# Attention scores of two steps issued together, with the low half of the queries in pairs of 64-row matmuls

## The chip, the cores and the metric

One core of one Trainium2 chip. The time is device microseconds of the whole program, the median of several runs. TensorE (PE in the profile) does the matmuls, its weight loads are shown as PEld, VectorE is DVE, ScalarE is ACT, GpSimd is POOL, and SP is the engine whose queue issues every DMA of this kernel.

## The reference

Three stages in a row. Squared-ReLU attention over two sequences of 3008 rows, then two feed-forward layers of 256 x 2048 x 256 over the 6016 rows:

```python
scores = (1/S) * z @ z.T                  # z: (2, 3008, 64)
attn = maximum(scores, 0) ** 2
x = u * (attn @ v)                        # u, v: (2, 3008, 256)
h = x @ w_in;  g = P(h) / (Q(|h|) + 1e-6) # rational, cubic over quadratic
y = g @ w_out
h = y @ w2_in; out = maximum(0.01 * h, h) @ w2_out
```

The weights arrive as 64-bit floats, and the kernel turns them into 32-bit ones itself.

## The kernel before

Every product is made in fp32r, with each operand split into a high part and a low part (the remainder), so that a product is the sum of two or three matmuls.

**Steps.** Attention runs in steps `t`. A block `i` of 512 queries (448 for the last of a sequence) takes 12 steps, one for each pair of 128-key blocks; there are 12 blocks, so 144 steps, and `t = 12 i + pair`. In one turn of the loop the program issues `scores(t)` (four matmuls of 512 columns on PE, then Relu and Square on ACT: tiles `sc`, `r` or `extra`, `ph`), then `av(t - 2)` (twelve matmuls, tile `oT`), then on DVE `square(t)` (line 232: r = r*r) and `square_low(t)` (line 238: the low part `pl`), and then the tasks that were registered for step `t`. The order on each engine is the order in which the program is written. The PSUM tile `sc` has two buffers, `r` and `ph` three, `pl` two.

**Keys and queries.** z has 64 columns. `prep_z` transposes 1024 rows of z on PE into a tile with the 64 columns twice, on partitions 0 to 63 and 64 to 127; ACT copies it (line 141) and DVE replaces the lower half by the remainder (line 142). So a key block holds the high part on one half of the partitions and the low part on the other. `prep_sq(i)` builds the queries of block `i` out of those keys by four DMAs (line 187): `queries[., 0]` holds the high part on both halves, `queries[., 1]` the low part on both halves. `scores` multiplies the key block (128 partitions) once by each. `first_z` does this for the first 512 rows, without DMAs.

**Tasks between the steps.** `prep_sq(i)` is registered for step 12 i - 4, `load_u`/`prep_u` (transposes `uTp` of u on PE, line 207, and a copy on ACT, line 209) for steps 12 i + 6 and 12 i + 10. The 32 pieces of weights are converted one every 3.4 steps, each over several steps from `s0 = 3 + k*17//5`: `load_w(k)` at step s0 - 1 (a DMA on SP, lines 279 and 282), `conv1` at s0 + 1 (ACT, line 287, and POOL), `conv2` to `conv4` at s0 + 2 to s0 + 4 (DVE, lines 294 to 303), `conv5` at s0 + 5 (ACT, line 315, POOL, line 316, and for the second layer's weights a store on SP, line 318). From step m0 = 119 on, the steps are merged with the first feed-forward layer; after step 145 only the two layers run.

The lines that tie the tasks to the steps:

```python
at(i * NPAIR - 4, lambda i=i: prep_sq(i))
...
halves = [(2 * (k // 16) + k % 2, (k % 16) // 4, (k % 4) // 2) for k in range(32)]
for k in range(32):
    s0 = 3 + k * 17 // 5
    for dt, f in ((-1, load_w), (1, conv1), (2, conv2), (3, conv3), (4, conv4), (5, conv5)):
        at(s0 + dt, lambda f=f, k=k: f(k))
```

By this rule `load_w(23)` stands at step 80 and `load_w(30)` at step 104, each right behind a `prep_sq` of the same step, and their `conv1` at steps 82 and 106.

Of the kernel before, what the change touches and what calls it, by code (L numbers as in the profile page):

```python
# [12 lines left out]
AF = mybir.ActivationFunctionType  # L13
ALU = mybir.AluOpType
# [3 lines left out]
def f32(ap):  # L18
    return ap.bitcast(F32)
# [3 lines left out]
def squared_relu_attention_moe_moe2(  # L23
# [14 lines left out]
    pe, act, dve, pool, sp = nc.tensor, nc.scalar, nc.vector, nc.gpsimd, nc.sync  # L38
# [4 lines left out]
    P = 128  # L43
    QB = 512
# [3 lines left out]
    NPAIR = KB // 2  # L48
# [3 lines left out]
    blocks = []  # L52
# [12 lines left out]
    def big(name):  # L65
        return ps.tile([P, 2, QB], F32, tag="big", name=name)
# [7 lines left out]
    def idle_acc(i, name):  # L74
        return acc(1 - own_acc(i), name)
# [43 lines left out]
    def key_chunk(c):  # L119
        return keys[c // 2][:, c % 2, :]  # L120

    def load_z(b, c, k0=0, k1=8):
# [7 lines left out]
                    sp.dma_start(t[h * KTAIL : (h + 1) * KTAIL, f1 - f0, d, :], z[b, f1 * P : S, :])  # L130
        return t

    def turn_z(pf, t, n):
        for k in range(n):
            pe.transpose(pf[:, k * P : (k + 1) * P], t[:, k, :, :].rearrange("p a d -> p (a d)"), ident)

    def prep_z(b, c, t, i):
        pf = idle_acc(i, f"zT{b}_{c}").rearrange("p a b -> p (a b)")
        turn_z(pf, t, 8)
        m = key_chunk(c)  # L140
        act.activation(m, pf, AF.Copy)
        dve.tensor_tensor(out=m[64:, :], in0=pf[64:, :], in1=f32(m[64:, :]), op=ALU.subtract)  # L142

    def first_z(ts):
        pf = idle_acc(0, "zT0_0").rearrange("p a b -> p (a b)")
        pg = big("zT0_0b").rearrange("p a b -> p (a b)")
        m, q = key_chunk(0), queries[0]
        for _ in range(WARM):
            pe.matmul(pg[:, :P], ident, ident, start=True, stop=True)
        turn_z(pf, ts[0], 4)  # L150
        act.activation(q[:, 0, :], pf[:, :QB], AF.Copy)
        turn_z(pg, ts[1], 4)
        dve.tensor_tensor(out=m[64:, :QB], in0=pf[64:, :QB], in1=f32(q[64:, 0, :]), op=ALU.subtract)
        act.activation(m[:64, :QB], f32(q[:64, 0, :]), AF.Copy)
        dve.tensor_tensor(out=q[:, 1, :], in0=pf[:, :QB], in1=f32(q[:, 0, :]), op=ALU.subtract)
        act.activation(m[:, QB:], pg[:, :QB], AF.Copy)
        dve.tensor_tensor(out=m[64:, QB:], in0=pg[64:, :QB], in1=f32(m[64:, QB:]), op=ALU.subtract)

    def load_v(b, c):
        t = raw_slot(f"vraw{b}_{c}", (P, 4, D))  # L160
# [20 lines left out]
    def prep_sq(i):  # L181
        b, q0, n = blocks[i]
        o = q0 % 1024
        m = key_chunk(q0 // 1024)[:, o : o + n]
        for h in range(2):
            for d in range(2):
                sp.dma_start(f32(queries[i % 2][d * 64 : (d + 1) * 64, h, :n]), f32(m[h * 64 : (h + 1) * 64, :]))

    uraw, uT, pacc = {}, {}, {}

# [21 lines left out]
    xs = [tc.dram_tile([P, 2, blocks[i][2]], F32, name=f"xs{i}") for i in range(NB)]  # L212
    R, PH, PL = {}, {}, {}

    def scores(t):
        i, pr = divmod(t, NPAIR)
        b, q0, n = blocks[i]
        s = big(f"sc{t}")
        for e in range(2):
            kb = 2 * pr + e  # L220
            o = (kb % 8) * P
            m = key_chunk(kb // 8)[:, o : o + P]
            for h in range(2):
                pe.matmul(s[:, e, :n], m, queries[i % 2][:, h, :n], start=h == 0, stop=h == 1)  # L224
        r = (extra[0] if t % 3 == 2 else slot(t % 3, f"r{t}"))[:, :, :n]
        act.activation(r, s[:, :, :n], AF.Relu, scale=SCALE)  # L226
        ph = slot(4 + t % 3, f"ph{t}", F32R)[:, :, :n]
        act.activation(ph, r, AF.Square)  # L228
        PH[t], R[t] = ph, r
# [99 lines left out]
    def at(step, f):  # L329
        tasks.setdefault(step, []).append(f)  # L330
# [49 lines left out]
    def load_x(i):  # L380
        n = blocks[i][2]
        if i >= 2 and i % 2 == 0:
            m = rtile(8, f"x1_{i}")
            xh, xl = (m[:, k, :].rearrange("p (a b) -> p a b", a=2) for k in range(2))
        else:
            xh, xl = slot(11, f"x1h{i}", F32R), slot(9, f"x1l{i}", F32R)
        sp.dma_start(f32(xl[:, :, :n]), xs[i])
        X1[i] = (xh, xl)
# [187 lines left out]
    TAIL = NC - NP  # L576
    MERGED = NP + 1
    m0 = NT + DEPTH - 3 * MERGED
    at(m0 - 4, lambda: load_x(0))
    at(m0 - 2, lambda: split_x1(0))  # L580
    at(m0 - 1, lambda: split_x1_low(0))
# [7 lines left out]
    for t in range(NT + DEPTH):  # L589
        c, ph = divmod(t - m0, 3)  # L590
        c = c if t >= m0 and c < MERGED else None
        if t < NT:
            scores(t)
        if c is not None and ph == 0:
            m1_h(c)
        if c and ph == 1:
            m1_y(c - 1, (0, 1, 2))
        if t >= DEPTH:
            av(t - DEPTH)
        if t < NT:  # L600
            square(t)
        if c is not None and ph == 0:
            m1_tb(c)
            m1_s(c)
            m1_v(c)
            m1_w(c)
            m1_q(c)
        if t < NT:
            square_low(t)
        for f in tasks.pop(t, []):  # L610
            f()
        if c is not None and ph == 1:
            m1_r(c)
            if c == NP:
                split_x2(0)
            m1_gh(c)
            m1_back(c)
        if c is not None and ph == 2:
            m1_gl(c)
# [97 lines left out]
```

## Time and profile before

| | |
|---|---|
| median of 3 runs | 1607.09 us (1605.28 to 1607.85) |
| the profiled execution | 1606.98 us, of which the span of its instructions is 1605.2 us |
| mean granted TensorE clock | 0.997 of 2.4 GHz |
| PE / DVE / ACT / POOL busy | 1581.3 / 1438.3 / 1098.6 / 165.4 us |
| attention alone (steps 0 to 118) | the first 457 us of the span |
| steps merged with the first layer | about 457 to 590 us |

The busy time of PE is a union of matmuls whose ends are modelled, so 100% does not say that it issues at its full rate; the distance between the starts of two groups does. A wait is shown in brackets behind the instruction that waited, with what released it. SPq rows are the DMA issues on the SP queue, with the time that the issue took on SP.

### The profile page before, as it was taken

How to read it: one execution, taken by the hardware profiler on the slowest of the kernel's cores; microseconds unless marked ns; L12 is line 12 of the kernel's file. 1: busy time of each engine (PE TensorE's matmuls, PEld its weight loads, DVE VectorE, ACT ScalarE, POOL GpSimd, SP SyncE). 2: the span in 40 equal slices, each digit the busy share in tenths (PEclk: the TensorE clock that was granted, in tenths of full speed). 3: DMA queues.
4: the chain of work that ended last, by engine and by line, in shares of the span. 5: the costliest groups of instructions: out<-in, count | busy, mean ns of one | idle time of the engine just before them, and what ended most of it. 6: DMA issues, size and time to landing. Idle time of an engine off the chain costs nothing.

```text
span 1605.2 us, 17951 instructions
## 1 busy us (share of the span) xinstructions
PE 1581.3 (99%) x7140; PEld 1323.7 (82%) x7140; DVE 1438.3 (90%) x1231; ACT 1098.6 (68%) x1109; POOL 165.4 (10%) x86
## 2 busy tenths in 40 slices
PE   8999999999999999999999999999999999999998
PEld 6788888788878887888888888888888888888887
DVE  7999999999979989999999998899999999999852
ACT  6666666666667766677777677777767676777643
POOL 2433335433200000000000000000000000000000
PEclk9999999999999999999999999999999999999999
DMA  6223236343220132000000000000000000000000
GB/s 170 66 67 87 84 90 178 115 137 119 92 68 23 56 113 104 13 14 14 14 1 12 13 13 14 13 14 13 12 14 14 13 14 1 25 1 0 14 1 25
DMA packets 51555, 74.42 MB, mean 46 GB/s; under 512 B 15632, under 2 KB 35344, under 8 KB 50448
## 3 DMA queue, kind: packets, MB, share of 16 engines
q1 hardware_dynamic: 51472, 73.28, 14.8%
q8 instruction: 56, 0.92, 0.2%
q14 instruction: 27, 0.22, 0.0%
HBM read 46.93 MB, written 20.71 MB: 42 GB/s over the span
## 4 chain that ended last, share of the span: by engine, by line
PE 85%; DVE 11%; issue 2%; ACT 2%; DMA 1%; DVEq 0%; POOL 0%; POOLq 0%; ACTq 0%
PE h L418 31%; PE y L432 31%; PE oT L257 16%; PE sc L224 5%; DVE pl L238 3%; DVE r L232 2%; DVE extra L232 1%; PE y L538 1%; DVE extra L303 1%; DVE extra L299 0%; PE uTp L207 0%; DVE t L464 0%; DVE extra L298 0%; DVE keys L142 0%; DVE t L459 0%
## 5 line engine op out<-in xcount | busy, mean ns | idle before, releaser
L432 PE MATMUL y<-gh,w 128*128 128x512 f32 (+1 forms) x1536 | 374.2, 386 | 0.7 <-DVE gh L475 0.5
L432 PEld LDWEIGHTS y<-gh,w 128*128 128x128 f32 x1536 | 288.2, 188 | 55.0 <-PE h L418 0.9
L257 PE MATMUL oT<-ph,V 128*128 128x512 f32 (+1 forms) x1128 | 276.3, 387 | 0.0
L257 PEld LDWEIGHTS oT<-ph,V 128*128 128x128 f32 x1128 | 212.9, 189 | 40.4
L432 PE MATMUL y<-gl,w 128*128 128x512 f32 (+1 forms) x768 | 203.3, 386 | 2.1 <-DVE gl L514 1.9
L418 PE MATMUL h<-x2h,w 128*128 128x512 f32 (+1 forms) x768 | 204.1, 388 | 0.0
L507 ACT ACTIVATE gh<-h 128x1024 fp32r<-128x1024 f32 (+1 forms) x96 | 97.0, 1011 | 143.1 <-PE y L432 125.1
L449 ACT ACTIVATE t<-h,par 128x1024 f32<-128x1024 f32 (+1 forms) x91 | 100.1, 1100 | 128.9 <-PE h L418 128.8
L432 PEld LDWEIGHTS y<-gl,w 128*128 128x128 f32 x768 | 144.1, 188 | 30.4 <-DVE gl L514 2.3
L418 PEld LDWEIGHTS h<-x2h,w 128*128 128x128 f32 x768 | 144.2, 189 | 26.2
L257 PE MATMUL oT<-pl,V 128*128 128x512 f32 (+1 forms) x576 | 153.7, 389 | 7.2 <-DVE pl L238 6.8
L459 DVE SCALAR_TENSOR_TENSOR t<-t,par,t 128x1024 f32<-128x1024 f32 (+1 forms) x91 | 114.6, 1259 | 46.0 <-ACT t L452 46.0
L238 DVE TENSOR_TENSOR pl<-r,ph 128x1024 fp32r<-128x1024 f32 (+1 forms) x96 | 139.7, 1455 | 9.1
L514 DVE TENSOR_TENSOR gl<-g,gh 128x1024 fp32r<-128x1024 f32 (+1 forms) x96 | 114.9, 1197 | 29.5 <-ACT g L509 29.5
L257 PEld LDWEIGHTS oT<-pl,V 128*128 128x128 f32 x576 | 107.1, 188 | 32.8 <-DVE pl L238 13.4
L468 ACT ACTIVATE t<-t,par 128x1024 f32<-128x1024 f32 (+1 forms) x91 | 103.4, 1136 | 36.9 <-DVE t L459 36.9
L475 DVE SCALAR_TENSOR_TENSOR gh<-t,par,t 128x1024 fp32r<-128x1024 f32 (+1 forms) x91 | 114.7, 1260 | 15.3 <-PE y L432 3.0
L226 ACT ACTIVATE r<-sc 128x1024 f32<-128x1024 f32 (+1 forms) x96 | 96.3, 1003 | 46.8 <-PE sc L224 45.1
L232 DVE TENSOR_TENSOR r<-r 128x1024 f32<-128x1024 f32 (+1 forms) x96 | 120.5, 1255 | 3.9 <-ACT ph L228 3.9
L483 DVE SCALAR_TENSOR_TENSOR t<-t,par,t 128x1024 f32<-128x1024 f32 (+1 forms) x96 | 121.1, 1262 | 3.1
L464 DVE SCALAR_TENSOR_TENSOR t<-t,par,h 128x1024 f32<-128x1024 f32 (+1 forms) x96 | 120.8, 1259 | 3.4
L418 PE MATMUL h<-x1h,w 128*128 128x512 f32 (+1 forms) x448 | 117.4, 384 | 2.7 <-DVE t L464 2.5
(92 smaller groups left out, 2468.9 us busy)
## 6 DMA issues: line engine op xcount, KB each, us to landing
wraw<-in_moe_w_in_dram SPq DMA_DIRECT2D x16, 512.0 KB, 4.9
wraw<-in_moe_w_out_dram SPq DMA_DIRECT2D x16, 512.0 KB, 4.1
w2s<-wst SPq DMA_DIRECT2D x16, 512.0 KB, 3.7
w<-w2s SPq DMA_DIRECT2D x8, 1024.0 KB, 4.9
vraw<-in_v_dram SPq DMA_DIRECT2D x10, 512.0 KB, 6.1
u<-in_u_dram SPq DMA_DIRECT2D x10, 512.0 KB, 5.2
xs<-u SPq DMA_DIRECT2D x10, 512.0 KB, 4.4
out_dram<-yo SPq DMA_DIRECT2D x10, 512.0 KB, 2.9
```

The costliest lines, as they stand in the source:

```text
L232: dve.tensor_tensor(out=R[t], in0=R[t], in1=R[t], op=ALU.mult)
L238: eng.tensor_tensor(out=pl, in0=r, in1=f32(ph), op=ALU.subtract)
L257: pe.matmul(a[:, j, :n], vt[:, h, o : o + P], mv[:, e, :], start=pr == 0 and si == 0 and e == 0, stop=pr == NPAIR - 1 and si == 2 and e == 1)
L418: pe.matmul(h[:, e, :n], w[:, hl, o : o + P], mv[:, k, :n], start=si == 0 and k == 0, stop=si == 2 and k == 1)
L432: pe.matmul(a[:, j, :n], w[:, hl, o : o + P], mv[:, e, :], start=p == 0 and si == 0 and e == 0, stop=p == NP - 1 and si == 2 and e == 1)
L449: act.activation(T[c]["t1"], T[c]["h"], AF.Abs, scale=b0)
L459: dve.scalar_tensor_tensor(out=d["t2"], in0=d["t2"], scalar=b1, in1=d["t1"], op0=ALU.mult, op1=ALU.add)
L464: dve.scalar_tensor_tensor(out=d["t3"], in0=d["t3"], scalar=ca[1], in1=d["h"], op0=ALU.add, op1=ALU.mult)
L468: act.activation(d["t1"], d["t2"], AF.Ln, scale=LSH, bias=lnb)
L475: dve.scalar_tensor_tensor(out=m1_tile(c, "gh", 14, F32R), in0=d["t3"], scalar=ca[0], in1=d["t1"], op0=ALU.add, op1=ALU.mult)
L483: dve.scalar_tensor_tensor(out=d["t3"], in0=d["t3"], scalar=ca[0], in1=d["t2"], op0=ALU.add, op1=ALU.subtract)
L514: dve.tensor_tensor(out=d["gl"], in0=d["g"], in1=f32(d["gh"]), op=ALU.subtract)
```

## The change

Odd key blocks are now stored with their halves swapped: an even block has the high part on partitions 0 to 63 and the remainder below, an odd block the other way round. The new helper `remainders` writes them with two DVE instructions in place of one, and `prep_sq` fetches the queries in pieces of 128 columns, since the halves alternate: 16 DMAs of 64 rows x 128 columns for a block, where there were four of 64 x 512.

`scores` now takes two steps. For an even `t` below 118 it issues the four matmuls with the queries' high part for both steps, and then the four with the low part, each on the 64 partitions that hold the key's high part only (so the product of the two low parts is no longer added in these steps). The even block's matmul lies on partitions 0 to 63, the odd block's on 64 to 127, so that two neighbours use different halves of the array. From step 118 on the steps are alone and all rows are used, as before. Relu and Square stay in the turn of their own step (`weigh`).

```diff
@@ -130,6 +130,14 @@
                     sp.dma_start(t[h * KTAIL : (h + 1) * KTAIL, f1 - f0, d, :], z[b, f1 * P : S, :])
         return t
 
+    def remainders(m, src, high):
+        for odd in range(2):
+            rows = slice(64 * (1 - odd), 64 * (2 - odd))
+            o, a, h = (x[rows, :].rearrange("p (k c) -> p k c", c=P)[:, odd::2, :] for x in (m, src, high))
+            dve.tensor_tensor(out=o, in0=a, in1=f32(h), op=ALU.subtract)
     def turn_z(pf, t, n):
         for k in range(n):
             pe.transpose(pf[:, k * P : (k + 1) * P], t[:, k, :, :].rearrange("p a d -> p (a d)"), ident)
@@ -139,7 +147,7 @@
         turn_z(pf, t, 8)
         m = key_chunk(c)
         act.activation(m, pf, AF.Copy)
-        dve.tensor_tensor(out=m[64:, :], in0=pf[64:, :], in1=f32(m[64:, :]), op=ALU.subtract)
+        remainders(m, pf, m)
 
     def first_z(ts):
         pf = idle_acc(0, "zT0_0").rearrange("p a b -> p (a b)")
@@ -150,11 +158,11 @@
         turn_z(pf, ts[0], 4)
         act.activation(q[:, 0, :], pf[:, :QB], AF.Copy)
         turn_z(pg, ts[1], 4)
-        dve.tensor_tensor(out=m[64:, :QB], in0=pf[64:, :QB], in1=f32(q[64:, 0, :]), op=ALU.subtract)
-        act.activation(m[:64, :QB], f32(q[:64, 0, :]), AF.Copy)
+        act.activation(m[:, :QB], f32(q[:, 0, :]), AF.Copy)
         dve.tensor_tensor(out=q[:, 1, :], in0=pf[:, :QB], in1=f32(q[:, 0, :]), op=ALU.subtract)
+        remainders(m[:, :QB], pf[:, :QB], q[:, 0, :])
         act.activation(m[:, QB:], pg[:, :QB], AF.Copy)
-        dve.tensor_tensor(out=m[64:, QB:], in0=pg[64:, :QB], in1=f32(m[64:, QB:]), op=ALU.subtract)
+        remainders(m[:, QB:], pg[:, :QB], m[:, QB:])
 
     def load_v(b, c):
         t = raw_slot(f"vraw{b}_{c}", (P, 4, D))
@@ -182,9 +190,12 @@
         b, q0, n = blocks[i]
         o = q0 % 1024
         m = key_chunk(q0 // 1024)[:, o : o + n]
-        for h in range(2):
-            for d in range(2):
-                sp.dma_start(f32(queries[i % 2][d * 64 : (d + 1) * 64, h, :n]), f32(m[h * 64 : (h + 1) * 64, :]))
+        for k in range(-(-n // P)):
+            c = slice(k * P, min((k + 1) * P, n))
+            for h in range(2):
+                r = 64 * ((h + k) % 2)
+                for d in range(2):
+                    sp.dma_start(f32(queries[i % 2][d * 64 : (d + 1) * 64, h, c]), f32(m[r : r + 64, c]))
 
     uraw, uT, pacc = {}, {}, {}
 
@@ -212,16 +223,31 @@
     xs = [tc.dram_tile([P, 2, blocks[i][2]], F32, name=f"xs{i}") for i in range(NB)]
     R, PH, PL = {}, {}, {}
 
-    def scores(t):
-        i, pr = divmod(t, NPAIR)
-        b, q0, n = blocks[i]
-        s = big(f"sc{t}")
-        for e in range(2):
-            kb = 2 * pr + e
-            o = (kb % 8) * P
-            m = key_chunk(kb // 8)[:, o : o + P]
-            for h in range(2):
-                pe.matmul(s[:, e, :n], m, queries[i % 2][:, h, :n], start=h == 0, stop=h == 1)
+    SC = {}
+    def scores(ts):
+        i = ts[0] // NPAIR
+        n = blocks[i][2]
+        q = queries[i % 2]
+        mm = []
+        for t in ts:
+            pr = t % NPAIR
+            SC[t] = big(f"sc{t}")
+            for e in range(2):
+                o = (2 * pr % 8 + e) * P
+                mm.append((SC[t][:, e, :n], key_chunk(pr // 4)[:, o : o + P], slice(64 * e, 64 * (e + 1))))
+        for s, m, h in mm:
+            pe.matmul(s, m, q[:, 0, :n], start=True, stop=False)
+        for s, m, h in mm:
+            h = h if len(ts) > 1 else slice(0, P)
+            pe.matmul(s, m[h, :], q[h, 1, :n], start=False, stop=True)
+    def weigh(t):
+        n = blocks[t // NPAIR][2]
+        s = SC.pop(t)
         r = (extra[0] if t % 3 == 2 else slot(t % 3, f"r{t}"))[:, :, :n]
         act.activation(r, s[:, :, :n], AF.Relu, scale=SCALE)
         ph = slot(4 + t % 3, f"ph{t}", F32R)[:, :, :n]
@@ -576,6 +602,7 @@
     TAIL = NC - NP
     MERGED = NP + 1
     m0 = NT + DEPTH - 3 * MERGED
+    assert m0 % 2 == 1
     at(m0 - 4, lambda: load_x(0))
     at(m0 - 2, lambda: split_x1(0))
     at(m0 - 1, lambda: split_x1_low(0))
@@ -590,7 +617,11 @@
         c, ph = divmod(t - m0, 3)
         c = c if t >= m0 and c < MERGED else None
         if t < NT:
-            scores(t)
+            if t >= m0 - 1:
+                scores([t])
+            elif t % 2 == 0:
+                scores([t, t + 1])
+            weigh(t)
         if c is not None and ph == 0:
             m1_h(c)
         if c and ph == 1:
```

On PE, in block 2 (steps 30 to 32), the program before issues the scores of one step between two groups of twelve (`oT`, x8 and x4):

```order
L224 MATMUL sc_1007<-sq,keys_70 128x512 x4
L257 MATMUL oT_906<-ph_960,V_2_257 128x512 x8
L257 MATMUL oT_906<-pl_975,V_2_257 128x512 x4
L224 MATMUL sc_1034<-sq,keys_70 128x512 x4
L257 MATMUL oT_906<-ph_986,V_2_257 128x512 x8
L257 MATMUL oT_906<-pl_1001,V_2_257 128x512 x4
L224 MATMUL sc_1063<-sq,keys_71 128x512 x4
```

The program with the change at the same place (L243 is the pass with the high part, L246 the pass with 64 rows; a row does not show how many rows a matmul has):

```order
L243 MATMUL sc_1035<-sq,keys_70 128x512 x2
L243 MATMUL sc_1036<-sq,keys_70 128x512 x2
L246 MATMUL sc_1035<-sq,keys_70 128x512 x2
L246 MATMUL sc_1036<-sq,keys_70 128x512 x2
L283 MATMUL oT_939<-ph_993,V_2_265 128x512 x8
L283 MATMUL oT_939<-pl_1008,V_2_265 128x512 x4
L283 MATMUL oT_939<-ph_1014,V_2_265 128x512 x8
L283 MATMUL oT_939<-pl_1029,V_2_265 128x512 x4
L243 MATMUL sc_1091<-sq,keys_71 128x512 x2
```

The scores of the odd step have moved ahead of the even step's `oT` group, and two `oT` groups now stand side by side.

On SP, at step 80, the queue before (`w2s<-wst` is the store of a converted piece, `keys<-keys` the queries of block 7, `wraw` the load of piece 23):

```order
L195 DMA u_2484<-in_u_dram 128x4x256
L318 DMA w2s_1_93<-wst_2514 256x1x512
L187 DMA keys_71<-keys_70 64x512 x4
L282 DMA wraw_2548<-in_moe_w_out_dram 128x2x512
L318 DMA w2s_1_89<-wst_2609 256x1x512
```

The same place with the change:

```order
L206 DMA u_2568<-in_u_dram 128x4x256
L344 DMA w2s_1_93<-wst_2593 256x1x512
L198 DMA keys_71<-keys_70 64x128 x16
L308 DMA wraw_2644<-in_moe_w_out_dram 128x2x512
L344 DMA w2s_1_89<-wst_2705 256x1x512
```

Nothing has changed places; between the store and the load of piece 23 there are 16 issues instead of four. The queue reads alike at step 104, with piece 30.

## Rows read from the trace of the kernel before

**Rows 1.** Stretches: us, PE, PEld, DVE, ACT, POOL busy, clock, DMA share, GB/s.
```profile
20.00:413.00 393.00, 383.43 (x1725) 316.35 (x1724) 377.95 (x341) 265.91 (x290) 152.02 (x73) 0.99 0.36 107
...
100.00:120.00 20.00, 20.00 (x90) 16.55 (x89) 19.48 (x20) 13.05 (x15) 6.93 (x4) 1.00 0.16 53
```

**Rows 2.** Waits of DVE from 20 to 445 us: us in total, times, longest.
```profile
DVE extra L232 <- ACT ph L228: 5.3, 3, 2.8
```

**Rows 3.** Timeline of PE: one step where PE never waits.
```profile
114.35 1.07 PE L224 MATMUL sc<-sq,keys 128*128 128x512 f32 x4
...
117.98 1.07 PE L224 MATMUL sc<-sq,keys 128*128 128x512 f32 x4
```

**Rows 4.** Timeline of PE and PEld: transposes of u, with and without two 64-row ones.
```profile
412.83 1.03 PE L207 MATMUL uTp<-ident,u 128*128 128x128 f32 x8
413.62 0.71 PE L224 MATMUL sc<-sq,keys 128*128 128x512 f32 x2
...
584.05 1.08 PE L207 MATMUL uTp<-ident,u 128*128 128x128 f32 x8
584.80 0.20 PEld L207 LDWEIGHTS uTp<-ident,u 64*128 64x128 f32 x2 [0.17 <-issue]
585.07 1.08 PE L224 MATMUL sc<-keys 128*128 128x448 f32 x4
```

**Rows 5.** The start: DVE and PE rows, and the first Relu on ACT.
```profile
5.84 0.69 DVE L153 TENSOR_TENSOR keys<-zT,sq 64x512 fp32r<-64x512 f32 x1 [5.84 <-ACT sq L151]
6.69 3.90 PE L224 MATMUL sc<-sq,keys 128*128 128x512 f32 x8 [0.31 <-DVE keys L153]
9.00 1.02 ACT L226 ACTIVATE r<-sc 128x1024 f32<-128x1024 f32 x1
```

**Rows 6.** Three lines by source: durations ns min/median/max.
```profile
L142 DVE TENSOR_TENSOR keys<-zT,keys x4: 1228/1228/1228, 36.7 to 307.9; 64x1024 fp32r<-64x1024 f32 x4
...
L187 SPq DMA_DIRECT2D sq<-keys x20: 467/588/1215, 83.7 to 447.8; - x20
...
L130 SPq DMA_DIRECT2D zraw<-in_z_dram x8: 587/595/3058, 12.5 to 294.8; - x8
```

**Rows 7.** Timeline of SP at steps 80 and 104, and the landing time of one load.
```profile
319.08 0.53 SPq L318 DMA_DIRECT2D w2s<-wst  x1
319.70 2.72 SPq L187 DMA_DIRECT2D keys<-keys  x4
322.52 0.54 SPq L282 DMA_DIRECT2D wraw<-in_moe_w_out_dram  x1
...
405.15 2.75 SPq L187 DMA_DIRECT2D keys<-keys  x4
...
wraw<-in_moe_w_out_dram SPq DMA_DIRECT2D x16, 512.0 KB, 4.1
```

**Rows 8.** Timeline of ACT and DVE around `conv1` of steps 82 and 106.
```profile
327.42 0.63 ACT L315 ACTIVATE wst<-extra 128x512 fp32r<-128x512 f32 x1 [0.41 <-DVE extra L303]
327.95 0.66 ACT L287 ACTIVATE cvc<-wraw 128x512 f32<-128x512 f32 x1
329.55 1.06 ACT L228 ACTIVATE ph<-extra 128x1024 fp32r<-128x1024 f32 x1
330.65 1.60 DVE L232 TENSOR_TENSOR extra<-extra 128x1024 f32<-128x1024 f32 x1
...
415.34 0.66 ACT L287 ACTIVATE cvc<-wraw 128x512 f32<-128x512 f32 x1
418.04 1.22 DVE L232 TENSOR_TENSOR extra<-extra 128x1024 f32<-128x1024 f32 x1 [2.76 <-ACT ph L228]
```

**Rows 9.** A load that came late (ACT), and what a PE pause did (PE, then a stretch).
```profile
313.71 0.68 ACT L287 ACTIVATE cvc<-wraw 128x512 f32<-128x512 f32 x1 [4.58 <-DMA wraw<-in_moe_w_in_dram]
...
272.08 1.07 PE L257 MATMUL oT<-pl,V 128*128 128x448 f32 x4 [2.48 <-DVE pl L238]
...
274.00:276.00 2.00, 2.00 (x9) 1.51 (x8) 1.90 (x3) 1.93 (x3) 1.25 (x1) 0.50 0.00 0
```

## The prediction, made before the change was run

> **What bounds the kernel now.** I read the shares of the engines first: PE 99%, DVE 90%. That is an average over attention and two layers, and the change touches steps 0 to 117 alone. So I took the stretch of those steps: from 20 to 413 us PE is busy 383 us, and DVE 378 of 393 [rows 1]. Both look full. In the piece from 100 to 120 us PE is never idle, and DVE is busy 19.48 of 20 [rows 1]. Which of the two has room is told by the waits of DVE: from 20 to 445 us it waited 5.3 us for `ph` in three waits, and next to nothing else [rows 2]. The rest of its idle time is the gap of some 0.1 us that every instruction shows. So in this stage DVE has 5 us to give, and no more, whatever PE does: two elementwise passes of each step and four conversion passes of each weight piece lie on it, and none of them goes away. PE is the pacemaker only in the stretches where one step follows the other in 3.63 us without a wait: 16 matmuls of 0.227 us [rows 3]. There DVE keeps up with it by a hair.
>
> **The change, part by part.**
>
> *PE.* In a pair of steps four full second-pass matmuls become four of 64 rows. If neighbours on the two halves overlap, two matmul times are saved, 0.45 us. The trace of before has no such pair. It has 64-row transposes, which show a cost: eight full transposes reach the next matmul in 0.79 us, 0.099 each; six full ones and two of 64 rows take 1.02 us, with a pause of the weight loader at the change [rows 4]. Six are 0.59; the two small ones cost between 0 and 0.20, so going to 64 rows and back costs 0.23 to 0.43 us. Each pair of steps does this once. What is left of the saving is 0.02 to 0.22 us for a pair; I take 0.12. The Trainium skill says so too (TensorEngine Tiling (Array Packing), Key Properties): a change of tiling mode drains the array; the pause in [rows 4] agrees. Without the drain the 59 pairs would save 27 us of PE time, with it 7.
>
> *What PE's saving is worth.* Between 20 and 413 us DVE can use at most its 2.5 us of waits there (5.3 less the one of 2.8 at 418 us, which is treated below) [rows 2]. I take -2. From step 107 to 117 the conversions thin out and PE paces: 11 steps of 0.06 us, -0.7; bounds 0 and -2.4 (0.22 us for every step).
>
> *Start.* The first scores waited for one DVE instruction of 0.69 us and started at 6.69 us. Now they need the queries' remainder (0.69) and two key pieces of 256 columns, each between 0.35 (half of such a row) and 0.69: 0.7 to 1.4 us later. And step 0 is complete only after five or six matmuls of the slow start instead of four (eight took 3.90 us, 0.49 each): 0.5 to 1.0 more. The scores were ready at 8.65 us, and Relu began at 9.00, so 0.35 is spare [rows 5]. That makes +0.85 to +2.05, say +1.3; from there DVE runs without a wait for over 100 us, so it is not won back.
>
> *Keys.* In the five later `prep_z` one DVE instruction of 1.228 us [rows 6] becomes two of 64 x 512, for which 0.69 stands in [rows 5]: 0.15 us each, +0.8 together, on a full DVE; bounds 0.5 and 1.2.
>
> *SP's queue.* This is the largest term, and no arithmetic unit shows it. `prep_sq` issues 16 DMAs where it issued four. One issue takes 0.588 us of SP at the median [rows 6], whatever lies behind it on the queue. Does it get shorter with a quarter of the columns? The nearest rows are the loads of the tail of z: 64 rows of 256 bytes, an eighth of the data, and the median issue is 0.595 us [rows 6]. So I take no shortening: 16 issues are 9.4 us by the median, 11.0 by the 2.75 us that four take at the places that matter [rows 7].
>
> In most blocks SP runs ahead and waits anyway. From block 6 on it doesn't: the stores of converted pieces (line 318) hold it until POOL has finished one. At step 80 the order is store, queries, load of piece 23. The queries start at 319.70 and the load left at 322.52 [rows 7], to be read by `conv1` at 327.95 [rows 8]. Now the load leaves at 329.1 to 330.7. It lands 4.1 us later at the median [rows 7], and at most 5.4, since the one at 322.52 was there at 327.95. So `conv1` starts at 333.2 to 336.1: 5.3 to 8.1 us late, say 6.5. Has ACT so much in hand? The `conv5` ahead of it had just waited for DVE itself, and the `ph` of step 83, queued behind `conv1`, ended at 330.61; DVE took it at 330.65, with no time between [rows 8]. So the whole delay becomes a wait of DVE. What else is queued behind: Relu of step 83, which frees the PSUM buffer that the scores of step 85 need, so PE stops as well; and the queries of block 7 land in the same microseconds.
>
> At step 104 the same three stand in a row: 405.15 plus 9.4 to 11.0, plus 4.1 to 5.4, is 418.65 to 421.55, where `conv1` started at 415.34: 3.3 to 6.2 us late, say 4.8. There DVE was already waiting 2.76 us behind it [rows 8], so this adds fully, and those 2.76 us are not won.
>
> *PE's clock.* At both places PE pauses 3 to 5 us. After a pause of 2.48 us before 272 us the granted clock read 0.50, that is 1.2 GHz, from 274 to 276 us [rows 9]. The next six or seven matmul times of scores would then cost 0.23 us more each, 1.5 us ahead of ACT and DVE; part is hidden by work in hand. +1 at each place, +2; bounds 0 and 4.
>
> **Sum.** -2 - 0.7 + 1.3 + 0.8 + 6.5 + 4.8 + 2 = +12.7 us. On the profiled execution, 1606.98 us (1605.2 of span and 1.8 around it), this gives 1619.7; the median of the runs, 1607.09, stands 0.1 above that execution, so 1619.8. With all low bounds +5.0 (1612), with all high bounds +21 (1628).
>
> **Rivals.**
>
> *The queue is not late.* If an issue of a quarter of the columns took well under its row, the load of piece 23 would be there in time: 8.25 us from 319.70 to 327.95, less 4.1 to 5.4 for landing, leave 0.18 to 0.26 us for each of 16. Then the terms of SP and of the clock go, and what stays is -0.6, or -3.4 if the wait of 2.8 at 418 us goes too: 1603.7 to 1606.5. For it: the load of 128 full rows takes SP 0.54 us, a little less than these [rows 7]. Against: the row of 0.595 us for less data. 17 in 100, of which 7 end below 1603.9. With issues of 0.35 us (5.6 us for 16) the load of step 80 is 1.5 to 2.8 us late and that of step 104 hardly: about 1609; 8 in 100.
>
> *PE sets the pace and the saving arrives.* 59 pairs of 0.45 us, without a cost of switching, give 1580; with it 1600. It needs DVE to do its work in less time, and the 378 of 393 us speak against it. The skill's page TensorE: Matmul & The Clock Gate (Part 3, The mechanism) has matmuls on different row strips start some 4 ns apart, which would make the pair cost one matmul time; no run here shows that yet. 5 in 100.
>
> *The pairs don't overlap.* Then nothing is saved and the switches remain, 0.33 us for a pair. Some 70 steps are paced by PE, so 35 pairs cost 11.6 us, of which some 3 lie under the two stalls, and the 2.7 us of gains go: about 1631. Nothing in the trace of before tells it apart. 10 in 100.
>
> **How the numbers follow.** The forecast, queue late at both places, has 60 in 100 and gives 1620. The range for 8 in 10 is 1604 to 1629: it takes in nearly all of the forecast and the two cases of a timely or nearly timely queue, and leaves out the full saving, most of the case without overlap, and tails. A difference under 0.2% (3.2 us) can't be told from none here. Faster: 5 + 7 = 12. Same: 10 + 7 of the queue's cases = 17. Slower: 71.
>
> **What would show it.** In the profile after: `prep_sq` x16 on SP taking 9 to 11 us; ACT waiting at `conv1` of steps 82 and 106 for a `wraw` load by about 5 to 8 and 3 to 6 us, followed by waits of DVE for `ph`, PE idle, and a dip of the clock; elsewhere DVE as full as before, and PE with idle time at `pl` instead of the 3.63 us rhythm. The four 64-row matmuls should take some 0.45 us plus the switches. Wrong would be: issues under 0.3 us; ACT finding the load in time; or DVE busy time in the stage falling or rising by several us, because its instructions meet POOL's at other moments, which no row bounds.

## The result, and the profile after

The changed kernel takes 1630.96 us (median, 1627.11 to 1632.99), the kernel before 1606.77 beside it: a ratio of 1.0148, 95% interval 1.0128 to 1.0169, or 24 us more. The forecast was +12.7, 1619.8, with a range from 1604 to 1629. The sign was right, the size about half. One of e6's executions and one of the kernel before beside it ran in a slower state and are left out of the times below.

The page of the profiled execution (1630.8 us, span 1629.0) gives the engines' busy time and share of the span, then the shares of the chain that ended last:

```profile
PE 1589.9 (98%) x7140; PEld 1297.4 (80%) x7140; DVE 1434.0 (88%) x1238; ACT 1095.8 (67%) x1109; POOL 166.6 (10%) x86
...
PE 82%; DVE 10%; ACT 3%; issue 3%; SPq 1%; POOL 1%; DMA 1%; DVEq 0%; ACTq 0%; POOLq 0%
```

DVE's work is about what it was (1438.3 before): the time did not come from more work on it. "SPq 1%" is new, since the chain of before had no SP in it: the issue of transfers is now on the path that sets the end.

**Where the time went.** For each step I subtracted the start of its Relu on ACT in the profile of before from that in the profile of another kernel. A row shows how far behind (+) that kernel is when the step begins, in us, and at the end of the span. The first row is the change; the others are experiments below. Each row is a single profiled execution, and its end need not be the median (that of e2 is 3.4 us above).

| kernel | step 0 | 24 | 60 | 80 | 88 | 104 | 112 | 140 | end |
|---|---|---|---|---|---|---|---|---|---|
| changed | 0.6 | 3.1 | 3.5 | 5.2 | 15.4 | 15.3 | 22.5 | 22.0 | 23.8 |
| e2, 16 transfers alone | 0.0 | 0.0 | 0.0 | -0.2 | 7.0 | 6.8 | 10.6 | 10.0 | 14.2 |
| e4, paired order alone | 1.1 | 5.2 | 5.8 | 6.1 | 8.3 | 8.3 | 8.6 | 8.2 | 7.3 |
| e15, both of these | 1.3 | 4.2 | 4.8 | 5.2 | 14.2 | 14.2 | 20.8 | 20.3 | 21.0 |
| e12, changed, queries earlier | 0.8 | 3.3 | 3.7 | 5.5 | 7.6 | 7.5 | 7.7 | 7.2 | 6.4 |
| e11, paired, one step's four matmuls first | 0.2 | 0.8 | 1.5 | 2.6 | 3.0 | 3.1 | 3.0 | 3.0 | 3.5 |

Three places in the changed kernel: +3.1 by step 24, +10.2 between steps 80 and 88, +7.2 between 104 and 112. Of the second, some 2.2 us stand in e4 and e12 too, where no load is late: they belong to the paired order. At the end 1.8 come on top, behind attention (last section). There the code is the same in all rows, and still they move by -0.9 (e4) to +4.2 us (e2).

SP at steps 80 and 104, which answers to [rows 7] (start, duration, engine, line, what it issues, count):

```profile
325.21 10.44 SPq L198 DMA_DIRECT2D keys<-keys  x16
335.75 0.53 SPq L308 DMA_DIRECT2D wraw<-in_moe_w_out_dram  x1
...
420.49 10.43 SPq L198 DMA_DIRECT2D keys<-keys  x16
431.02 0.53 SPq L305 DMA_DIRECT2D wraw<-in_moe_w_in_dram  x1
```

Four issues took 2.72 and 2.75 us, 0.68 and 0.69 each; 16 of a quarter of the columns take 10.4, 0.65 each. The size makes an issue hardly shorter. What waits behind, on ACT and DVE, beside [rows 8]:

```profile
340.61 0.66 ACT L313 ACTIVATE cvc<-wraw 128x512 f32<-128x512 f32 x1 [5.37 <-DMA wraw<-in_moe_w_out_dram]
343.30 1.22 DVE L258 TENSOR_TENSOR extra<-extra 128x1024 f32<-128x1024 f32 x1 [7.95 <-ACT ph L254]
...
435.11 0.66 ACT L313 ACTIVATE cvc<-wraw 128x512 f32<-128x512 f32 x1 [3.96 <-DMA wraw<-in_moe_w_in_dram]
437.80 1.22 DVE L258 TENSOR_TENSOR extra<-extra 128x1024 f32<-128x1024 f32 x1 [7.16 <-ACT ph L254]
```

PE at the same places, and two stretches (us, PE, PEld, DVE, ACT, POOL busy, clock, DMA share, GB/s):

```profile
336.23 0.61 PE L243 MATMUL sc<-keys,keys 128*128 128x512 f32 x2
342.23 1.22 PE L243 MATMUL sc<-keys,keys 128*128 128x512 f32 x2 [5.39 <-DMA wraw<-in_moe_w_in_dram]
...
432.14 0.61 PE L243 MATMUL sc<-keys,keys 128*128 128x512 f32 x2
436.74 1.22 PE L243 MATMUL sc<-keys,keys 128*128 128x512 f32 x2 [3.98 <-ACT extra L252]
437.89 1.22 PE L246 MATMUL sc<-keys,keys 64*128 64x512 f32 x4
439.04 3.79 PE L283 MATMUL oT<-ph,V 128*128 128x512 f32 x8
...
342.00:348.00 6.00, 5.77 (x15) 3.78 (x16) 4.01 (x4) 4.23 (x5) 1.26 (x1) 0.52 0.04 16
437.00:443.00 6.00, 6.00 (x15) 3.91 (x16) 4.01 (x4) 3.84 (x5) 0.77 (x1) 0.50 0.13 49
```

In the pair the first step's two matmuls run, and the other step's two wait for ACT to free the second buffer of `sc`; the first step, whose buffer is free, waits with them. (At the first place the row names a load as what released PE; ACT's Relu, which frees the buffer, ends at 342.18, just before.) Behind pauses of 5.4 and 4.0 us the granted clock is 0.50, and eight `oT` matmuls take 3.79 us. The price of such a pause differs between executions: in e5, the same kernel again, the pause at the second place is 3.96 us, the clock from 438 to 444 us 0.72, and the eight matmuls take 2.81.

DVE's waits from 20 to 465 us, beside [rows 2], whose 20 to 445 us are about the same steps:

```profile
DVE extra L258 <- ACT ph L254: 22.7, 9, 8.0
DVE pl L264 <- PE oT L283: 5.9, 4, 2.0
DVE r L258 <- ACT ph L254: 3.6, 4, 2.8
```

One pair of steps on PE and its weight loader where nothing else waits, beside [rows 3]:

```profile
131.40 1.07 PE L243 MATMUL sc<-sq,keys 128*128 128x512 f32 x4
132.40 0.73 PE L246 MATMUL sc<-sq,keys 64*128 64x512 f32 x4
133.06 2.12 PE L283 MATMUL oT<-ph,V 128*128 128x512 f32 x8
...
138.64 1.07 PE L243 MATMUL sc<-sq,keys 128*128 128x512 f32 x4
...
132.40 0.30 PEld L246 LDWEIGHTS sc<-sq,keys 64*128 64x128 f32 x4 [0.35 <-issue]
133.06 1.69 PEld L283 LDWEIGHTS oT<-ph,V 128*128 128x128 f32 x8 [0.36 <-issue]
```

From 131.40 to 138.64 are 7.24 us, where two steps took 2 x 3.63 = 7.26 [rows 3]: the pair brings 0.02. 24 pairs of the changed kernel stand 7.24 apart, and pairs of e4, with 128 rows, 7.25. Neighbours do overlap: two of the four 64-row matmuls start together at 132.4, the other two at 132.7. Four 64-row matmuls reach the next group in 0.66 us instead of 0.91, and still nothing is won: the loader stands still for 0.35 us when it goes to 64 rows and 0.36 when it comes back.

### The profile page after: what moved, and what is told of

It is laid out like the page before. It is cut to its first block, busy times and chain, and to the rows that moved or that the text cites. A ratio compares the mean times of both kernels' runs of the same rounds, so it can differ in the third digit from the quotient of the medians.

```text
span 1629.0 us, 18164 instructions
## 1 busy us (share of the span) xinstructions
PE 1589.9 (98%) x7140; PEld 1297.4 (80%) x7140; DVE 1434.0 (88%) x1238; ACT 1095.8 (67%) x1109; POOL 166.6 (10%) x86
## 4 chain that ended last, share of the span: by engine, by line
PE 82%; DVE 10%; ACT 3%; issue 3%; SPq 1%; POOL 1%; DMA 1%; DVEq 0%; ACTq 0%; POOLq 0%
PE h L444 31%; PE y L458 31%; PE oT L283 14%; DVE pl L264 3%; PE sc L243 3%; PE sc L246 2%; DVE r L258 2%; DVE extra L258 1%; SPq L198 1%; ACT ph L254 1%; PE y L564 1%; DMA wraw<-in_moe_w_in_dram 1%; ACT r L252 1%; DVE extra L320 0%; DVE u L288 0%
## 5 line engine op out<-in xcount | busy, mean ns | idle before, releaser
L283 PE MATMUL oT<-ph,V 128*128 128x512 f32 (+1 forms) x1128 | 289.9, 400 | 0.0
L264 DVE TENSOR_TENSOR pl<-r,ph 128x1024 fp32r<-128x1024 f32 (+1 forms) x96 | 133.5, 1391 | 12.3 <-PE oT L283 3.4
L501 DVE SCALAR_TENSOR_TENSOR gh<-t,par,t 128x1024 fp32r<-128x1024 f32 (+1 forms) x91 | 114.7, 1260 | 15.3 <-PE y L458 3.0
```

The source lines that it names most:

```text
L264: eng.tensor_tensor(out=pl, in0=r, in1=f32(ph), op=ALU.subtract)
L283: pe.matmul(a[:, j, :n], vt[:, h, o : o + P], mv[:, e, :], start=pr == 0 and si == 0 and e == 0, stop=pr == NPAIR - 1 and si == 2 and e == 1)
L501: dve.scalar_tensor_tensor(out=m1_tile(c, "gh", 14, F32R), in0=d["t3"], scalar=ca[0], in1=d["t1"], op0=ALU.add, op1=ALU.mult)
```

## The experiments

Theory Q: the load behind the 16 issues comes late at two places, and that is the main cost. Rivals: the paired order itself (P), the swapped storage, row switches that cost more than they save.

**e1, the changed kernel with the queries of blocks 7 and 9 two steps earlier.** Those two `prep_sq` then stand ahead of other tasks, not right before the load.

```
-            at(i * NPAIR - 4, lambda i=i: prep_sq(i))
+            at(i * NPAIR - (6 if i in (7, 9) else 4), lambda i=i: prep_sq(i))
```

> The changed kernel, with the queries of blocks 7 and 9 fetched two steps earlier (at steps 78 and 102), so that their 16 issues fall into SP's wait for a store and the loads of pieces 23 and 30 leave on time. Theory Q (the late loads are the main cost: steps 84 to 86 and 108 to 110 lost 8.1 and 7.2 us against the kernel before): 15 us less than the changed kernel, 1613 to 1619. Theory P (the paired order of the scores is the main cost, and the late loads lie under it): 1625 to 1631.

It took 1616.72 us, ratio to before 1.0045 (1.0025 to 1.0066); run again as **e12**, 1613.72, 1.0036 (1.0024 to 1.0049). The changed kernel, run again as **e5** on the same chip as e6 to e8, took 1629.16, 1.0132 (1.0116 to 1.0148), a little less than the 22 us or more that were expected.

> The changed kernel once more, on the chip of the other three, as their measure: 22 to 26 us slower than the kernel before on it.

> The changed kernel with the queries of blocks 7 and 9 two steps earlier, once more, on the chip of the other three: 1614 to 1618.

So 14 to 16 of the 21 to 24 us hang on where two groups of 16 issues stand. On SP they take no less time than before, but they begin earlier (e12):

```profile
314.17 12.85 SPq L198 DMA_DIRECT2D keys<-keys  x16
...
327.77 0.56 SPq L308 DMA_DIRECT2D wraw<-in_moe_w_out_dram  x1
```

The load of piece 23 leaves 8 us sooner than in the changed kernel, and the table's row of e12 has no jump of 7 or 10.

**e2, the kernel before with the 16 transfers alone.** `prep_sq` copies 64x128 pieces instead of 64x512; nothing else changes.

```
+        for k in range(-(-n // P)):
+            c = slice(k * P, min((k + 1) * P, n))
...
-                sp.dma_start(f32(queries[i % 2][d * 64 : (d + 1) * 64, h, :n]), f32(m[h * 64 : (h + 1) * 64, :]))
+                    sp.dma_start(f32(queries[i % 2][d * 64 : (d + 1) * 64, h, c]), f32(m[h * 64 : (h + 1) * 64, c]))
```

> The kernel before, with only the queries' four DMAs of 64 x 512 split into 16 of 64 x 128; keys, scores and order as before. Theory Q: 1619 to 1623, 12 to 16 us slower than the kernel before, with the waits at the conversions of steps 82 and 106. Theory P: 1607 to 1611.

1617.78, 1.0055 (1.0037 to 1.0073): +9.6, less than Q expected (12 to 16) and more than P (at most 3). SP, ACT and PE at the first place, then PE at the second:

```profile
319.55 10.38 SPq L189 DMA_DIRECT2D keys<-keys  x16
330.03 0.53 SPq L284 DMA_DIRECT2D wraw<-in_moe_w_out_dram  x1
335.34 0.66 ACT L289 ACTIVATE cvc<-wraw 128x512 f32<-128x512 f32 x1 [7.44 <-DMA wraw<-in_moe_w_out_dram]
336.96 1.21 PE L226 MATMUL sc<-keys,keys 128*128 128x512 f32 x4 [2.02 <-ACT extra L228]
...
338.00:342.00 4.00, 4.00 (x11) 2.98 (x11) 3.86 (x4) 3.94 (x5) 0.00 (x1) 0.57 0.00 0
...
428.68 1.19 PE L226 MATMUL sc<-keys,keys 128*128 128x512 f32 x4 [0.89 <-ACT extra L228]
...
428.00:436.00 8.00, 6.39 (x26) 4.74 (x27) 6.00 (x7) 5.84 (x7) 1.72 (x1) 1.00 0.14 54
```

The load and ACT are as late as foreseen. In the old order PE's pauses are shorter. At the first place they are 0.7 and 0.8 us for the queries themselves, which land late too, and 2.0 us for ACT; the clock still falls, to 0.57 from 338 to 342 us, and the place costs 7.2 us. At the second place a pause is 0.9 us at a time, the clock stays at 1.00, and the place costs 3.8 us, against 7.2 in the changed kernel.

**e4, the kernel before with the paired order alone** (all passes with 128 rows, four transfers).

```
...
+        for s, m, h in mm:
+            pe.matmul(s, m, q[:, 0, :n], start=True, stop=False)
+        for s, m, h in mm:
+            h = slice(0, P)
+            pe.matmul(s, m[h, :], q[h, 1, :n], start=False, stop=True)
...
+            elif t % 2 == 0:
+                scores([t, t + 1])
...
```

> The kernel before, with only the order changed: the scores of two steps together, high parts of both first, all with 128 rows; keys and the four DMAs as before. Theory Q leaves 3 to 8 us for it (both PSUM buffers must be free before any score of the pair can be finished): 1610 to 1615. Theory P: 1617 to 1625. If the order costs nothing: 1605 to 1609.

1613.5, 1.0033 (1.0023 to 1.0043): +5.3. The prediction had no term for it but at the start. Steps 0 and 1, then 2 and 3, on PE, then PE's waits for ACT from 12 to 465 us:

```profile
9.02 1.91 PE L235 MATMUL sc<-sq,keys 128*128 128x512 f32 x4
...
11.58 0.71 PE L232 MATMUL sc<-sq,keys 128*128 128x512 f32 x2
13.19 0.73 PE L232 MATMUL sc<-sq,keys 128*128 128x512 f32 x2 [0.90 <-ACT r L241]
13.76 1.08 PE L235 MATMUL sc<-sq,keys 128*128 128x512 f32 x4
...
PE sc L232 <- ACT r L241: 4.7, 7, 1.1
PE sc L232 <- ACT extra L241: 2.6, 2, 2.3
```

The first two matmuls at 11.58 need one buffer, the next two the other, for which PE waits 0.90 us; only then comes the second pass of the even step, which could have run at once. Such waits come nine times, 7.3 us together; in the kernel before PE's `sc` never waits for ACT there. The late start has a price of its own. At step 8 PE waits for DVE to write a key chunk's remainders: 2.22 us in the kernel before, 3.46 in e4, where DVE is still 1.1 us behind. From 40 to 44 us the clock is then 0.50, where it is 1.00 in the kernel before:

```profile
38.02 1.20 PE L224 MATMUL sc<-sq,keys 128*128 128x512 f32 x4 [2.22 <-DVE keys L142]
...
39.14 2.07 PE L232 MATMUL sc<-sq,keys 128*128 128x512 f32 x4 [3.46 <-DVE keys L142]
...
40.00:44.00 4.00, 4.00 (x10) 3.03 (x10) 3.72 (x4) 2.45 (x3) 2.78 (x1) 0.50 0.00 0
```

**e11, the same pairs, each step's four matmuls in turn.** If that wait is the cost, it must go. The edit against e4:

```
-        for s, m, h in mm:
-            pe.matmul(s, m, q[:, 0, :n], start=True, stop=False)
-        for s, m, h in mm:
-            h = slice(0, P)
-            pe.matmul(s, m[h, :], q[h, 1, :n], start=False, stop=True)
+        for j in range(0, len(mm), 2):
+            for h in range(2):
+                for s, m, _ in mm[j : j + 2]:
+                    pe.matmul(s, m, q[:, h, :n], start=h == 0, stop=h == 1)
```

> The paired order alone (128 rows, keys and DMAs as before), but within the pair the even step's four matmuls come first and the odd step's four after them. Theory C (the cost of the pairing is that the even step's scores are finished only behind the odd step's first pass, which needs the other PSUM buffer): 1608 to 1611. If it is the place of the odd step's scores, ahead of the even step's twelve matmuls: 1612 to 1616.

1609.86, 1.0015 (1.0006 to 1.0024): about half of it goes. In the table e4 loses 5.2 us by step 24, e11 0.8; its step 0 is 0.2 us late, PE waits 2.20 us at step 8, and the clock is 1.00 from 40 to 44 us. What is left may stand where `uTp` is transposed: ACT's copy of `u` waits for the transposes, with Relu queued behind it. In the kernel before these waits sum to 9.9 us in seven places from 20 to 460 us, in e4 to 13.4, in e11 to 14.3. One of them in e4, on ACT and DVE:

```profile
102.45 1.03 ACT L209 ACTIVATE u<-uTp 128x1024 f32<-128x1024 f32 x1 [1.79 <-PE uTp L207]
103.37 1.02 ACT L241 ACTIVATE extra<-sc 128x1024 f32<-128x1024 f32 x1
...
105.52 1.23 DVE L247 TENSOR_TENSOR extra<-extra 128x1024 f32<-128x1024 f32 x1 [1.51 <-ACT ph L243]
```

This second part is read from rows; no run took it away.

**e15, paired order and 16 transfers in the kernel before.** Do the two costs add, or do they meet?

> The kernel before with the paired order of scores (all passes with 128 rows, storage not swapped) and the queries copied by 16 transfers instead of 4. Alone the paired order gave +5.3 and the 16 issues +9.6. If the two add, the time is before + 14 to 16, 1621 to 1623. If the late queue costs more under the paired order, because PE then waits longer for a pair and its clock falls at both places, before + 18 to 22, 1625 to 1629, as the changed kernel, whose own parts (64 rows, swapped storage) then add nothing. Under 1620 would mean that the late queue's cost depends on the swapped storage.

1626.08, 1.0119 (1.0105 to 1.0133): +18.6, where the parts alone sum to 14.9. The difference of 3.7 is not clear of noise: the intervals are 16.9 to 21.4 for e15, 5.9 to 11.7 for e2 and 3.7 to 6.9 for e4. In the table the meeting is at the second place: 6.6 us from step 104 to 112 in e15, 3.8 in e2, 0.3 in e4. The rows of e15 there are those of the changed kernel:

```profile
435.52 1.22 PE L234 MATMUL sc<-keys,keys 128*128 128x512 f32 x2 [3.79 <-ACT extra L243]
...
436.00:440.00 4.00, 4.00 (x11) 3.03 (x11) 3.01 (x4) 2.89 (x4) 0.56 (x1) 0.50 0.15 57
```

The pair makes one pause of 3.8 us where the old order made small ones, and behind it the clock is 0.50 instead of 1.00. At the first place, where the clock fell in e2 as well, e15 loses 9.0 us, and e2 and e4 lose 7.2 and 2.2: no more than the parts. That the two costs meet is thus read from one place in single executions, and e5 shows that the clock behind such a pause can also be 0.72.

**e8, the changed kernel with 8 transfers instead of 16** (each takes two 128-column pieces with a stride): a dose.

```
...
+        for odd in range(2):
...
+                src = m[r : r + 64, :].rearrange("p (k c) -> p k c", c=P)[:, odd::2, :]
...
```

> The changed kernel, with the queries in 8 DMAs (all even blocks of a half in one, all odd ones in another) instead of 16. Theory Q by dose: 8 issues take some 5.2 us; the load of piece 23 is then 1 to 2.5 us late instead of 8, that of piece 30 in time or 0.5 late: 12 to 15 us less than the changed kernel on the same chip. If a delay of any size costs the same (a pause that drops the clock): 4 to 8 us less.

1615.27, 1.0043 (1.0027 to 1.0059): 13.9 less than e5. SP's row is halved with the count:

```profile
325.51 5.39 SPq L199 DMA_DIRECT2D keys<-keys  x8
```

With 5.4 us the load is in time: ACT's `conv1` of step 82 starts at 335.40 without a wait. The bytes are the same as with 16; what counts here is the number of issues.

**e3 and e10, 64 rows or 128.** e3 is the changed kernel, e10 is e1, each with `h = slice(0, P)` in the second pass.

> The changed kernel, with all 128 rows in the second pass (the product of the low parts comes back), so no change of rows in the array; pairs of steps, swapped halves and 16 DMAs stay. Theory S (two switches eat the whole saving of a pair): no difference, 1628 to 1634, with 7.25 us from pair to pair instead of 7.24. If 64 rows save something: 1634 to 1640. If the switches cost more than they save: below 1628.

> The changed kernel with the queries of blocks 7 and 9 two steps earlier, and with all 128 rows in the second pass. Beside the next one it prices the 64 rows without a late queue. Theory S': the switches cost a little more than the pairs save, so 1 to 4 us less than the next one, 1612 to 1616. If the 64 rows save something once the queue is out of the way: 1617 to 1622.

e3: 1627.0, 1.0111 (1.0095 to 1.0128), 2 to 4 less than the changed kernel. e10: 1615.2, 1.0049 (1.0037 to 1.0062), 1.5 more than e12. e3 was expected at 1628 to 1634, e10 at 1 to 4 less than e12; neither came. The signs differ: nothing that can be told from none.

**e6, e4 with 64 rows on the same half for both blocks of a pair.** Without the swapped storage the high parts of both blocks lie on that half, so only the product of the two low parts is left out, as in the changed kernel. Neighbours then share a half of the array; the switches stay.

> The kernel with the paired order alone (keys and four DMAs as before), with its second pass on partitions 0 to 63 for the even and the odd block, which hold the high parts of both (the product of the low parts is left out in the paired steps, as in the changed kernel). Neighbours share a half of the array and can't overlap. Theory O (in the changed kernel neighbours overlap, and the switches eat what that saves): the pair grows from 7.25 to about 7.7 us, so 8 to 16 us slower than the paired order alone, 1621 to 1630. If 64-row matmuls never overlap and are merely as long as full ones: 7.6 us in the changed kernel too, which its trace would have to show, and about 1621. If they are cheaper than full ones by themselves: 1613 to 1617.

1635.05, 1.0164 (1.0146 to 1.0183): +27 beside the kernel before, 22 more than e4, where 8 to 16 more were expected. One pair:

```profile
135.53 1.07 PE L232 MATMUL sc<-sq,keys 128*128 128x512 f32 x4
136.53 1.20 PE L235 MATMUL sc<-sq,keys 64*128 64x512 f32 x4
...
143.25 1.07 PE L232 MATMUL sc<-sq,keys 128*128 128x512 f32 x4
```

7.72 us for a pair, 0.48 more than with two halves, 0.46 more than without switches. So the overlap is real and gives 0.48. If four 64-row matmuls on one half take as long as four of 128 rows, the two switches cost 0.46.

**e7, swapped storage alone**: 16 transfers, placed as in e1, single steps with 128 rows.

> The kernel before with only the storage changed: odd key blocks with halves swapped (two DVE instructions in place of one), 16 DMAs for the queries, those of blocks 7 and 9 two steps earlier so that no load is late; scores step by step with 128 rows. The start and the keys alone, by the prediction 1.3 + 0.8: 1609 to 1611 beside 1608. If the 16 issues cost something in the other blocks too: 1612 or more.

1608.51, 1.0005 (0.9995 to 1.0015), or +0.8 us with bounds of -0.8 and +2.4: nothing that can be told from none.

**e9, e13, e14: does DVE set the pace?** e9 drops one conversion pass from DVE (the weights lose their signs). e13 and e14 leave nothing out and move squares from DVE to ACT, at every fourth step (below) or at two of twelve (`t % 12 in (3, 8)`):

```
+        if t < NT - 28 and t % 4 == 3:
+            act.activation(R[t], R[t], AF.Square)
+        else:
             dve.tensor_tensor(out=R[t], in0=R[t], in1=R[t], op=ALU.mult)
```

> The kernel before, with one of the four conversion passes on DVE left out for each of the 32 weight pieces (the one that puts the sign back, 0.69 us each, 22 us in all, so the weights lose their signs). Theory D (DVE sets the pace of the attention steps over long stretches): 4 to 10 us faster than the kernel before, up to where PE's 3.63 us for a step bind. If PE sets the pace: no difference, 1605 to 1609.

> The kernel before, with the square of every fourth step up to step 115 on ScalarE (28 of 116) instead of VectorE. Theory D (VectorE's work paces the stage, ScalarE has room): each moved square takes some 1.2 us off VectorE; after the earlier run that took work from VectorE gave back only 3 to 4 us, because TensorE then paces, I expect 2 to 6 us less than before, 1601 to 1605. Rival: ScalarE works in order, the square of 1 us holds up the next Relu or the high part behind it, and the time is the same or longer, 1606 to 1616.

> The same with only two squares of every twelve steps on ScalarE, at the steps where VectorE takes part in a conversion. Theory D: 1 to 5 us less than before, 1602 to 1606, and closer to the run with 28 squares than in proportion to their number, because TensorE is the next bound. Rival (ScalarE in order holds up the chain): the same or some us longer, 1606 to 1612.

e9: 1603.71, 0.9973 (0.9962 to 0.9983), 3.4 us less, just under the 4 to 10 expected. e13: 1600.27, 0.9956 (0.9944 to 0.9969), 7 us less than before, a little more than expected, and the fastest of all kernels here. e14: 1603.28, 0.9972 (0.9963 to 0.9981). From 20 to 413 us in e13, with DVE's largest wait, beside [rows 1]:

```profile
20.00:413.00 393.00, 386.02 (x1762) 320.85 (x1761) 346.80 (x318) 296.12 (x324) 156.06 (x75) 1.00 0.37 109
...
DVE pl L241 <- ACT extra L233: 16.4, 8, 4.1
```

DVE has 31 us less to do, and the kernel gains 7; PE is busy 386 of 393, and DVE waits for the squares on ACT. DVE did hold PE back, by some 7 us as far as these runs show.

**e16 and e17: the pairs with DVE relieved.** e12 with e13's squares on ACT; e17 is its twin with 128 rows.

> The changed kernel with the queries of blocks 7 and 9 two steps earlier, and with the square of every fourth step up to step 115 on ScalarE. VectorE has then some 30 us to give in the stage, as in the run of the kernel before with these squares. Theory W (the row switches cost on TensorE what the 64-row pairs save): the same time as its twin with 128 rows, within 2 us, some 1606 to 1610. Rival D (the pairs save TensorE time, but VectorE could not follow): 4 to 13 us less than the twin, 1594 to 1603.

> Its twin: the same kernel with 128 rows in the second pass. Under both theories it is the base of the comparison: the early queries stood at before + 7, the squares on ScalarE gave 7 in the kernel before, so about the time of the kernel before, 1605 to 1610.

1609.34, 1.0015 (1.0007 to 1.0024), and 1611.22, 1.0023 (1.0013 to 1.0033). The intervals overlap, and the 1.9 us between them are far from the 4 to 13 that a saving on PE would have brought. The 64 rows have nothing to give that can be told from none, even when DVE could follow.

## Why the prediction was wrong

The step that failed is that the paired order was put at nothing behind the start: it costs 5.3 us by itself (e4), where the sum has only the 1.3 of the start. Two terms were mis-sized beside it: PE's saving of 2.7 us did not come, and the pauses with the clock behind them cost 1 to 3 us more than the sum has.

- **SP's queue.** Right in mechanism and nearly in size. 9.4 to 11.0 us were forecast for 16 issues, 10.4 were measured; no shortening, as taken. ACT found the load late at both places; alone this costs 9.6 us (e2, bounds 5.9 and 11.7, with what the clock costs there), where the terms of 6.5 and 4.8 make 11.3.
- **The clock.** Priced too low. The term was +2, bounds 0 and 4. The pauses of 3 to 5 us that were forecast came as 5.4 and 4.0. Behind them 342 to 348 and 437 to 443 us stand at 0.52 and 0.50, and eight `oT` matmuls take 3.6 and 3.8 us instead of 2.0; the prediction had priced six or seven slow matmuls of scores alone. The queue with the clock came to 14 to 16 us (changed against e1, e5 against e12) where 13.3 stood in the sum.
- **The paired order.** This is the missing term: +5.3 (e4). The prediction saw at the start that step 0 is complete only after more matmuls, and then wrote that from there DVE runs without a wait for over 100 us. It did not carry the thought on: every pair asks for both buffers of `sc` at once, so wherever ACT has not yet read the odd step before it, the even step waits too: nine times in e4, 7.3 us on PE. The later start also makes PE's wait for keys at step 8 longer, 3.46 us for 2.22, and the clock falls behind it. In e11 most of both is gone, and with it about half of the cost; the other half was taken away by no run. By step 24 the changed kernel is 3.1 us behind, where +1.3 was forecast for the start and at most 0.8 for all keys.
- **PE's saving.** -2.7 was forecast and nothing came. Overlap: right, 0.48 for a pair (e6), where 0.45 was taken. Switches: 0.46 (e6), where I took 0.33 between 0.23 and 0.43; the net is 0.02 and not 0.12. The Trainium skill (TensorEngine Tiling (Array Packing), Key Properties) says that a change of tiling mode drains the array; the trace agrees, with 0.35 and 0.36 us of a standing loader. Had I taken the upper bound, the term would have been right. The rival "the pairs don't overlap" had the time right (1631) by luck: e6, where neighbours share a half, has 7.72 us for a pair, and the changed kernel 7.24.
- **DVE paces the stage, PE has little room behind it.** Right in part: with 31 us taken off DVE, the kernel before gains 7 (e13), and PE is then busy 386 of 393. The prediction's gap of some 0.1 us at every DVE instruction is misread: from 20 to 413 us 15 us of idle time and 3.4 of waits leave 0.03 for each of 341. But DVE was not what denied the saving: with DVE relieved the 64 rows give nothing that can be told from none (e16 against e17).
- **Start and keys**, +2.1: the storage alone costs 0.8 (e7, not told from none). The start came through the paired order: step 0 is 1.1 us late in e4, 0.6 in the changed kernel, and early by 0.8 in e7. The two key instructions of 512 columns take 0.69 us each for one of 1.228, as forecast.
- **What stays open.** e15 stands at +18.6, the changed kernel at +21 to +24. Of these 3 to 5 us some 1.8 lie behind attention in the profiled execution of the changed kernel (below), but only 0.2 in that of e5; e3 is 2 to 4 under the changed kernel, e10 above its twin, so I can't lay the rest on the 64 rows.

The sum with the measured terms: 9.6 (late load alone) + 5.3 (paired order) + 3.7 (their meeting, e15, not clear of noise) + 0.8 (storage) + 0 (PE) = 19.4, to which 2 to 5 us are missing without a cause that a run shows.

## What to carry to other kernels

Count the issues of a change before its bytes, and look at which load stands right behind them on that queue; moving two groups of transfers by two steps was worth 15 us here. Where a change lets two steps share a group of instructions, ask which buffers the whole group now needs at once, and how long a pause becomes when small ones are put together. And cost a saving against the upper bound of what it brings along: here two row switches ate two overlapped matmuls to within 0.02 us.

## What I had not expected of the hardware

- Two row switches, with 512-column passes on either side, cost 0.46 us in a pair of steps (e6 against 7.26, if the 64-row matmuls of e6 are as long as full ones), as much as two matmuls.
- The issue of a 64x128 transfer takes SP as long as one of 64x512 (0.65 against 0.68 and 0.69 at these places), and one of a strided 64-row piece with two runs of 128 columns too (0.67).
- The same pause has not the same effect in every execution. PE waits 2.5 us for DVE behind attention in both kernels; in the profile of before the four `h` matmuls behind it take 1.17 us, in that of the changed kernel 1.55, at a clock of 0.57. In e5, the same kernel again, PE waits 2.55 us there, the four take 1.16, and the clock is 1.00 (second stretch):

```profile
633.94 1.55 PE L444 MATMUL h<-x1h,w 128*128 128x512 f32 x4 [2.52 <-DVE t L490]
...
634.00:638.00 4.00, 4.00 (x11) 3.13 (x12) 3.83 (x4) 1.54 (x2) 0.00 (x0) 0.57 0.74 309
...
634.00:638.00 4.00, 4.00 (x19) 3.29 (x19) 3.83 (x4) 2.59 (x4) 0.00 (x0) 1.00 0.74 307
```

This makes up most of the 1.8 us at the end, and it can move a run by that much without any difference in the code. In e2, which loses 4.2 us behind attention, the clock is 0.52 from 621 to 628 us.
